# Attention followed by two gated layers on one Trainium2 core: two PSUM tiles, an earlier key preparation, and a reordered end of the attention

## The chip, the cores and the metric

The kernel runs on one core of one Trainium2 chip. Its time is device microseconds of one execution, the median of several. A profile is one execution taken by the hardware profiler; its span runs from the first instruction of the program to the last.

## What is computed

The reference chains three parts: hashed attention, a gated linear layer, and a layer of eight experts of which each token uses one.

```python
def _attn_ref(q, k, v, proj):              # 2 batches, 8 heads, 768 rows, 64 columns
    q_bits = (einsum('bhsd,dk->bhsk', q, proj) > 0)      # 6 hash bits
    k_bits = (einsum('bhsd,dk->bhsk', k, proj) > 0)
    mask = bucket(q_bits)[:, :, :, None] == bucket(k_bits)[:, :, None, :]
    scores = where(mask, scale * q @ k.T, -1e9)
    attn = softmax(scores)                                # exp(scores - max) / (sum + 1e-9)
    return attn @ v
def _moe_ref(x, w_a, w_b, w_out):           # 1536 tokens, 512 wide, 1536 hidden
    return (x @ w_a) * (x @ w_b) @ w_out
def _moe2_ref(x, expert_emb, tau, w1, w2):  # 8 experts, 512 -> 1024 -> 512
    expert_idx = argmax(normalized(x) @ normalized(expert_emb).T / tau)
    out[mask] = gate_w[mask] * (maximum(x[mask] @ w1[e], 0) @ w2[e])
```

The three `w` matrices of the gated layer come as 64-bit floats and are split in the kernel into a high and a low part; products of high and low parts are summed.

## The kernel before

**Attention** goes by 8 pairs of heads (two heads side by side on the 128 partitions) and by 48 units, six to a pair: a unit is one head's 256 query rows, taken as two score tiles t = 0 and 1 of 128 rows by 768 keys. `units` (u) numbers them; `s = u % 3` is the place within a head and `r = u % 6` within a pair. Order within each engine is the program's order, written out by hand in the loop over u of `attention`.

For each score tile `scores` multiplies q by k (fp32, L180) and adds a product of hash signs (bf16, L182) that pushes pairs of other buckets far down. `rowmax` (VectorE, L187), `expo` (ScalarE, L193, out of PSUM, so that the score buffer is free again), `normal` (GpSimd, L202 to L206) and `turn` (VectorE, a 32x32 transpose, L213) follow. There are two score buffers in PSUM (`ps_s`, four banks). The weighted sum `pv` (L222) of a head is 192 small matmuls, in two halves of 96 in the units s = 0 and s = 1; it accumulates in the other four banks, one tile `pvb`. In the unit s = 2 `epilogue` copies its two partial results (partitions 0 to 63 and 64 to 127, L240) to the SBUF tiles `xp` and `co`; `finish_add` sums them, `finish_high` and `finish_low` split the sum into `xh` and `xl`.

The same tile `pvb` serves the preparation of later pairs, in units without a weighted sum. `turned` transposes raw q and k (L107; then copies to `Q` and `K` on ScalarE, L121, and DMAs that swap the two halves of the partitions, `QS` and `KS`, L127 and L129). `signs` makes the hash products of k (L156) and q (L150) and takes their signs (`sk` L161, `qf` L151). In the unit u both parts, k then q, are issued after the scores of the next unit's first tile; their results leave PSUM in unit u + 1 behind its first exponential. `turned` of pairs 2 to 7 runs in u = 5, 11, ..., 35 and of pair 1 in u = 1, `signs` of pair 1 in u = 3 and of pairs 2 to 7 in u = 8, 14, ..., 38. In u = 41 and 44, which have no preparation, the first two of sixteen half products of the gated layer run in `pvb`'s banks (L511, via `hook`, `fill` and `gated_products`), with their results taken at once by ScalarE (L519) or VectorE (L523).

`hook(u, at)` inserts jobs of the later stages at marked places of the unit: with `plan` and `places` the loading and splitting of the first weights (`load_first`: fetch, rest, top, low, add, size, guard, parts; L409 to L442), in the tile `spare` or `late`.

**The end of the attention**: after the loop the copies of head 14 follow, then two half products, the whole weighted sum of head 15, four hooks that split weights, the last copies and ten half products. `fin == 1` and `fin == 2` in the loop put the sum of pair 6 on GpSimd and its split on ScalarE and GpSimd.

**Later stages**: the gated layer goes by chunks of 256 hidden columns (`gated_products` L511, `gated_out` L537), with routing beside the last chunk, and the experts by `hidden_rows` (L849), `hidden` (L831) and `expert_out` (L881). `begin` gives the memory of `xh` and `xl` to a pool of the experts' tiles (`xgh`, `xgl`, `hs`, `hth`, `htl`, `o`), which take their places in order of first use.

Of the kernel before, what the change touches and what calls it, by code (L numbers as in the profile page):

```python
# [25 lines left out]
class Kernel:  # L26
# [37 lines left out]
    def attention(self, xh, xl, pools, hook):  # L64
# [9 lines left out]
        for tag, shape, dt, n in (  # L74
            ("et", [128, NC * S], F32, 2), ("e", [128, S], F32, 6), ("vr", [128, NC * 256], F32, 2), ("raw", [128, 2 * S], F32, 1),
            ("q", [128, S], F32, 2), ("qs", [128, S], F32, 2), ("k", [128, S], F32, 2), ("ks", [128, H2], F32, 2),
            ("xp", [128, S], F32, 2), ("co", [128, S], F32, 2), ("qf", [128, S], BF16, 2), ("kf", [128, S], BF16, 2), ("sk", [128, H2], BF16, 1),
        ):
            sb.tile(shape, dt, tag=tag, name=tag, bufs=n)
        raw, Q, QS, K, KS, QF, KF, VR = {}, {}, {}, {}, {}, {}, {}, {}  # L80
# [18 lines left out]
        pvb = ps_pv.tile([128, 4, 512], F32, tag="pv", name="pv")  # L99

        self.banks = pvb
        self.bank = lambda: ps_s.tile([128, 2, 512], F32, tag="s", name="part")[:, 0]

        def turned(i, n):
            p = pvb[:, 2 * n:2 * n + 2]
# [12 lines left out]
            def out(eng):  # L118
# [5 lines left out]
                for a in (1, 0):  # L124
                    x, y = slice(64 * a, 64 * a + 64), slice(64 - 64 * a, 128 - 64 * a)
                    if n == 0:
                        nc.sync.dma_start(out=QS[i][x], in_=Q[i][y])  # L127
                    else:
                        nc.sync.dma_start(out=KS[i][x], in_=K[i][y, a * H2:(a + 1) * H2])  # L129
# [14 lines left out]
        def signs(i, n):  # L144
            p = pvb[:, 2 * n:2 * n + 2]
            lz = self.lz.rearrange("p a b c -> p (a b c)")
            if n == 0:
                QF[i] = sb.tile([128, S], BF16, tag="qf", name="qf", bufs=2)
# [5 lines left out]
            for x in range(2):  # L154
                r = slice(64 * x, 64 * x + 64)
# [4 lines left out]
            def out(*_):  # L160
                nc.scalar.activation(sk, p[:, 0, :H2], AF.Sign, bias=self.bias, scale=2.0 ** 100)  # L161
# [10 lines left out]
        def scores(u, t):  # L172
# [8 lines left out]
            for n, d in enumerate(rows):  # L181
                nc.tensor.matmul(st[:, n, :H2], QF[i][d, ql], KF[i][d, j], start=False, stop=True, tile_position=(64 * n, 0))  # L182
# [32 lines left out]
        def pv(h, blocks):  # L215
            et, vr = ET[h], VR[h]
            for n in blocks:
                m = 64 * (n % 2)
                v = vr[:, n % 4, n // 4 * D:n // 4 * D + D]
                for a in range(4):  # L220
                    d = slice(32 * a, 32 * a + 32)
                    nc.tensor.matmul(  # L222
                        pvb[m:m + 64, a, :NC * 32], v[d], et[d, n].rearrange("p c s -> p (c s)"),
# [3 lines left out]
        def product(n, cs):  # L227
            return pvb[64 * n:64 * n + 64, :, cs.start * 32:cs.stop * 32].rearrange("p a (c s) -> p a c s", s=32)
# [3 lines left out]
        def place(i, n, j, cs):  # L232
            if i not in XP:
                XP[i] = [sb.tile([128, S], F32, tag=t, name=t, bufs=2) for t in ("xp", "co")]
            return XP[i][n][64 * j:64 * j + 64, cs.start * 128:cs.stop * 128].rearrange("p (c a s) -> p a c s", a=4, s=32)
# [3 lines left out]
        def epilogue(h, n):  # L239
            nc.scalar.copy(place(h // 2, n, h % 2, every), product(n, every))  # L240
# [18 lines left out]
        for m in range(22):  # L259
            nc.tensor.transpose(pvb[:, m % 2, m // 2 % 4 * 128:m // 2 % 4 * 128 + 128], self.ident, self.ident)  # L260
# [4 lines left out]
        turned(0, 1)(nc.scalar)  # L265
        turned(0, 0)(nc.vector)
# [16 lines left out]
        for u in range(NU + 2):  # L283
# [4 lines left out]
            new = len(pairs)  # L288
            if act:
# [12 lines left out]
            if preps and kind is turned and held + 1 < len(pairs):  # L302
# [16 lines left out]
            if u == 1 or s == 2 and r == 5:  # L319
                new, kind = 1 if u == 1 else (u + 7) // 6, turned  # L320
            elif u == 3 or s == 2 and u > 2:
                new, kind = 1 if u == 3 else i + 1, signs
            if new < len(pairs):
                preps, held = [kind(new, x) for x in (1, 0)], new
# [20 lines left out]
        for n in range(2):  # L345
            epilogue(2 * end, n)
        hook(NU + 2, 0)
        finish_add(end, slice(0, S), slice(0, 64), nc.vector)
        pv(2 * end + 1, range(NB32))
        for at in ((NU + 2, 4), (NU + 3, 3), (NU + 3, 4), (NU + 4, 3)):  # L350
            hook(*at)
        for g in range(2):
            cs = slice(3 * g, 3 * g + 3)
            nc.scalar.copy(place(end, 1, 1, cs), product(1, cs))
            nc.vector.tensor_tensor(place(end, 0, 1, cs), product(0, cs), place(end, 1, 1, cs), ALU.add)
# [4 lines left out]
        hook(NU + 3, 0)  # L360
# [17 lines left out]
class Experts:  # L378
# [115 lines left out]
    def gated_products(self, c, t, f, which, half, psum=None):  # L494
# [22 lines left out]
        if which == 0:  # L517
            self.A = self.mid.tile([128, 384], F32, tag="a", name="a")
            nc.scalar.copy(self.A, p[:, :384])  # L519
        else:  # L520
            a = self.A
# [728 lines left out]
```

## Time and profile before

| | us |
|---|---|
| median of three runs (754.02 to 756.55) | 754.89 |
| the profiled execution | 752.32 |
| its span | 750.5 |
| busy: TensorE, VectorE, ScalarE, GpSimd | 707.7, 460.7, 351.6, 439.4 |

Attention takes up the first 245 us or so, the gated layer and the routing go to about 560, the experts to the end. The mean granted clock of TensorE is 0.993 of full speed. Matmuls are pipelined, and a matmul's recorded time reaches into the next one, so a sum of mean times is more than the time that a stream of them takes. The chain of waits follows the work that ended last back from a stretch's end; in the timeline a bracket gives the engine's idle time and what ended it.

### The profile page before, as it was taken

To read this page: it belongs to the slowest core of one execution; us is meant where nothing else is said; L and a number is where in the kernel's file an instruction comes from. 1 tells how busy PE (TensorE), PEld (TensorE's weight loads), DVE (VectorE), ACT (ScalarE), POOL (GpSimd) and SP (SyncE) were. 2 spreads that over 40 slices of the span, in tenths; PEclk is the share of its full clock that TensorE was granted. 3 is DMA by queue.
4 is the path that set the end of the run, shared out by engine and by line. 5 is a ranking of instruction groups with operands and counts; after the bars stand their busy time and mean duration, and the time that the engine had idled before them with its cause. 6 is when DMAs were issued, how large, how long until landed. Compare 5 with 4: busy or idle time off the path is not lost.

```text
span 750.5 us, 16392 instructions
## 1 busy us (share of the span) xinstructions
PE 707.7 (94%) x6793; PEld 588.6 (78%) x6793; DVE 460.7 (61%) x675; ACT 351.6 (47%) x620; POOL 439.4 (59%) x453
## 2 busy tenths in 40 slices
PE   7699898998986999999999999999999999999996
PEld 4356555555655999999999999998888999889995
DVE  3889888988785462655545646533853865565650
ACT  2667777877654344121212122224535655555551
POOL 0666888888767364462654635643612866556651
PEclk9999999999999999999999999999999999999999
DMA  6854665354215031121220211154261876666610
GB/s 145 185 118 98 135 145 124 80 118 118 72 45 179 6 114 57 56 67 48 72 97 22 91 57 57 32 207 140 72 197 38 264 235 200 242 209 232 204 67 23
DMA packets 67485, 87.62 MB, mean 117 GB/s; under 512 B 28739, under 2 KB 40003, under 8 KB 67408
## 3 DMA queue, kind: packets, MB, share of 16 engines
q1 hardware_dynamic: 63200, 78.81, 37.4%
q0 software_dynamic: 2560, 7.34, 2.6%
q8 instruction: 54, 0.88, 0.5%
q10 hardware_dynamic: 1648, 0.39, 0.3%
q14 instruction: 23, 0.19, 0.1%
HBM read 75.52 MB, written 7.34 MB: 110 GB/s over the span
## 4 chain that ended last, share of the span: by engine, by line
PE 78%; DVE 6%; ACT 5%; POOL 4%; issue 4%; DMA 2%; SPq 0%; POOLq 0%; DVEq 0%; ACTq 0%
PE ab L511 24%; PE yp L537 13%; PE op L881 10%; PE hp L831 9%; PE pv L222 6%; PE st L180 5%; DVE nm L187 2%; ACT e L193 2%; POOL e L206 2%; DVE et L213 2%; PE hr L849 2%; PE part L511 1%; PE pv L150 1%; PE st L182 1%; PE xgt L808 1%
## 5 line engine op out<-in xcount | busy, mean ns | idle before, releaser
L511 PE MATMUL ab<-xh,w 128*128 128x384 f32 x704 | 185.7, 338 | 0.0
L511 PEld LDWEIGHTS ab<-xh,w 128*128 128x128 f32 x704 | 127.7, 188 | 2.1 <-issue 1.3
L525 POOL TENSOR_TENSOR g<-a,g 128x384 fp32r<-128x384 f32 x48 | 54.7, 1140 | 109.9 <-ACT g L524 109.8
L511 PE MATMUL ab<-xl,w 128*128 128x384 f32 x352 | 118.3, 336 | 0.0
L787 POOL TENSOR_TENSOR w<-raw,w 128x1024 fp32r<-128x1024 f32 x36 | 88.0, 2448 | 36.2 <-ACT w L786 35.1
L193 ACT ACTIVATE e<-st,nm 128x768 f32<-128x768 f32 x96 | 86.5, 901 | 44.9 <-DVE nm L187 22.8
L187 DVE TENSOR_REDUCE nm<-st 128x1 f32<-128x768 f32 x96 | 90.3, 942 | 24.4 <-PE st L182 24.1
L537 PE MATMUL yp<-w,g 128*128 128x512 f32 x432 | 102.9, 390 | 0.0
L206 POOL TENSOR_SCALAR e<-e,s,mc 128x768 f32<-128x768 f32 x96 | 95.7, 1005 | 5.4 <-POOL s L204 0.2
L180 PE MATMUL st<-ks,qs 64*128 64x384 f32 x192 | 85.1, 524 | 12.0 <-ACT e L193 12.0
L213 DVE STREAM_TRANSPOSE et<-e 128x768 f32<-128x768 f32 x96 | 92.5, 964 | 4.6 <-PE pv L222 1.0
L180 PE MATMUL st<-k,q 64*128 64x384 f32 x192 | 85.3, 524 | 10.4 <-ACT e L193 10.4
L537 PEld LDWEIGHTS yp<-w,g 128*128 128x128 f32 x432 | 80.4, 188 | 14.9
L881 PE MATMUL op<-w,hth 128*128 128x512 f32 x256 | 81.7, 400 | 0.0
L831 PE MATMUL hp<-xgh,w 128*128 128x256 f32 x448 | 80.7, 281 | 0.0
L222 PE MATMUL pv<-et,vr 32*64 32x192 f32 x3072 | 72.1, 330 | 8.0 <-ACT co L240 5.3
L222 PEld LDWEIGHTS pv<-et,vr 32*64 32x64 f32 x3072 | 60.9, 133 | 23.4 <-issue 8.1
L524 ACT CAST g<-a 128x384 fp32r<-128x384 f32 x48 | 24.8, 516 | 108.3 <-DVE a L523 108.3
L787 DVE TENSOR_TENSOR w<-raw,w 128x1024 fp32r<-128x1024 f32 x28 | 64.8, 2313 | 14.6 <-ACT w L786 14.3
L831 PEld LDWEIGHTS hp<-xgh,w 128*128 128x128 f32 x448 | 69.1, 188 | 0.3
L511 PEld LDWEIGHTS ab<-xl,w 128*128 128x128 f32 x352 | 66.2, 188 | 0.8
L786 ACT CAST w<-raw 128x1024 fp32r<-128x1024 f32 x64 | 66.1, 1044 | 0.0
(197 smaller groups left out, 1162.8 us busy)
## 6 DMA issues: line engine op xcount, KB each, us to landing
raw<-in_moe_w_dram SPq DMA_DIRECT2D x32, 1024.0 KB, 5.5
vr<-in_v_dram SPq DMA_DIRECT2D x64, 192.0 KB, 4.3
raw<-in_moe_w_a_dram SPq DMA_DIRECT2D x5, 1024.0 KB, 5.2
raw<-in_moe_w_b_dram SPq DMA_DIRECT2D x5, 1024.0 KB, 5.1
raw<-in_moe_w_out_dram SPq DMA_DIRECT2D x5, 1024.0 KB, 4.9
raw<-in_k_dram SPq DMA_DIRECT2D x16, 192.0 KB, 4.7
qs<-q SPq DMA_DIRECT2D x16, 192.0 KB, 4.1
ybuf<-y SPq DMA_DIRECT2D x12, 256.0 KB, 6.3
```

The costliest lines, as they stand in the source:

```text
L180: nc.tensor.matmul(st[:, n, :H2], q[d, ql], k[d], start=True, stop=False, tile_position=(64 * n, 0))
L187: nc.vector.tensor_reduce(NM[u][:, t:t + 1], ST[u, t][:, :, :H2], axis=AX.XY, op=ALU.max, negate=True)
L193: nc.scalar.activation(e, ST.pop((u, t))[:, :, :H2], AF.Exp, bias=NM[u][:, t:t + 1], accum_out=SU[u][:, t:t + 1])
L206: nc.gpsimd.tensor_scalar(E[u, t], E[u, t], r[:, t:t + 1], c[:, t:t + 1], ALU.mult, ALU.add)
L213: nc.vector.transpose(ET[h][:, :, c], E.pop((u, t)).rearrange("p a (b s) -> p (a b) s", s=32))
L222: nc.tensor.matmul(pvb[m:m + 64, a, :NC * 32], v[d], et[d, n].rearrange("p c s -> p (c s)"), start=(n < 2), stop=(n >= NB32 - 2), tile_pos ...
L511: nc.tensor.matmul(p[:, :384], w[:, k, fs], x[:, k, cols], start=(k == 0 and n == 0), stop=(k == self.KD - 1 and n == 2),)
L537: nc.tensor.matmul(p, g[:, f, rows], w[:, f], start=(n == 0), stop=(n == 5))
L786: nc.scalar.copy(h, raw)
L787: eng.tensor_tensor(l, raw, f32(h), ALU.subtract)
L831: nc.tensor.matmul(p[:, :256], w[:, k, fs], x[:, k], start=(n == 0), stop=(n == 3 * self.KD - 1))
L881: nc.tensor.matmul(p, h[:, 2 * n + f, rows], w[:, f], start=(n == 0 and f == 0 and m == 0), stop=(n == 3 and f == 1 and m == 2),)
```

## The change

Five things, all in the order and the places of work; what is computed stays the same.

1. `pvb` becomes a list of two tiles of two banks each. K's part of a preparation uses `pvb[1]`, q's part `pvb[0]`; the weighted sum uses both. `epilogue(h, g)` copies tile g, in two pieces of 64x384, so a head has four copies, g = 1 first.
2. Where copies and a preparation meet (u = 8, 11, ..., 38), k's part (`fresh`) is issued right behind the copies of tile 1, ahead of the scores of the next unit's first tile; q's part stays where it was.
3. Apart from pair 0, the hash products of q are made like k's, in two halves of 64 columns of the array, with one sign of 128x384 to `QF` and two DMAs on SP's queue that give the other order, `QG`. Pair 0 takes four signs of 64x384 and no DMA.
4. Pair 0's transposes are both issued before their copies, and its swaps alternate between k and q. The results of the half products in u = 41 and 44 are `held` until the middle of the next unit; two further half products run in u = 48. The conversion of the output weights moves: its first half three units ahead, its second half between the steps of the end. The end puts products between the halves of the last weighted sums and takes pair 6's split behind the copies.
5. `begin` allocates the experts' tiles beforehand, with 72 floats (`edge`) between `hs` and `hth` and 56 (`room`) behind `htl`.

```diff
@@ attention: banks, swaps
-        pvb = ps_pv.tile([128, 4, 512], F32, tag="pv", name="pv")
+        pvb = [ps_pv.tile([128, 2, 512], F32, tag=f"pv{n}", name="pv") for n in range(2)]
+        def swap(i, n, a):
+            x, y = slice(64 * a, 64 * a + 64), slice(64 - 64 * a, 128 - 64 * a)
+            if n == 0:
+                nc.sync.dma_start(out=QS[i][x], in_=Q[i][y])
+            else:
+                nc.sync.dma_start(out=KS[i][x], in_=K[i][y, a * H2:(a + 1) * H2])
@@ signs
-            p = pvb[:, 2 * n:2 * n + 2]
+            p = pvb[n]
-                for x in range(2):
-                    nc.tensor.matmul(p[:, x, :H2], lz, Q[i][:, x * H2:(x + 1) * H2], start=True, stop=True)
-                return lambda *_: nc.scalar.activation(halves(QF[i]), p[:, :, :H2], AF.Sign, bias=self.bias, scale=2.0 ** 100)
+                for x, r in enumerate(half):
+                    if i == 0:
+                        nc.tensor.matmul(p[:, x, :H2], lz, Q[i][:, x * H2:(x + 1) * H2], start=True, stop=True)
+                    else:
+                        nc.tensor.matmul(
+                            p[r, 0, :H2], lz[:, r], Q[i][:, x * H2:(x + 1) * H2], start=True, stop=True, tile_position=(0, 64 * x)
+                        )
+                def out(*_):
+                    if i == 0:
+                        for x in range(2):
+                            sign(QF[i][half[x]], p[half[x], x, :H2])
+                            sign(QG[i][half[1 - x]], p[half[1 - x], x, :H2])
+                        return
+                    sign(QF[i], p[:, 0, :H2])
+                    for x in range(2):
+                        nc.sync.dma_start(out=QG[i][half[1 - x]], in_=QF[i][half[x]])
@@ scores
+                qf = (QF if n == c // (NC // 2) else QG)[i][d, c % (NC // 2) * 128:c % (NC // 2) * 128 + 128]
@@ copies
-        def epilogue(h, n):
-            nc.scalar.copy(place(h // 2, n, h % 2, every), product(n, every))
+        def epilogue(h, g):
+            for n in range(2):
+                nc.scalar.copy(place(h // 2, n, h % 2, g, every), product(n, g, every))
@@ start
-        turned(0, 1)(nc.scalar)
-        turned(0, 0)(nc.vector)
+        turns = turned(0, 1), turned(0, 0)
+        turns[0](nc.scalar, False)
+        turns[1](nc.vector, False)
+        for a in (1, 0):
+            for n in (1, 0):
+                swap(0, n, a)
@@ loop over the units
-            moves = [((u - 8) // 3, n) for n in range(2)] if s == 2 and u >= 8 else []
+            moves = [((u - 8) // 3, g) for g in (1, 0)] if s == 2 and u >= 8 else []
             for m in moves[:2 if u == NU - 1 else 1]:
                 epilogue(*m)
+            if moves and new < len(pairs):
+                fresh.append(kind(new, 1))
...
-                preps, held = [kind(new, x) for x in (1, 0)], new
+                preps, held, held_kind = fresh + [kind(new, x) for x in (1, 0)[len(fresh):]], new, kind
...
-                    if fin == 1:
+                    if fin == 2:
                         finish_add(done, cols[g])
-                    if fin == 2:
-                        finish_high(done, cols[g])
-                        finish_low(done, cols[g])
@@ end
-        for n in range(2):
-            epilogue(2 * end, n)
+        for g in (1, 0):
+            epilogue(2 * end, g)
         hook(NU + 2, 0)
+        hook(NU + 2, 3)
+        pv(2 * end + 1, range(12))
         finish_add(end, slice(0, S), slice(0, 64), nc.vector)
-        pv(2 * end + 1, range(NB32))
-        for at in ((NU + 2, 4), (NU + 3, 3), (NU + 3, 4), (NU + 4, 3)):
-            hook(*at)
+        finish_high(end - 1, slice(0, S))
+        hook(NU + 2, 4)
+        hook(NU + 3, 0)
+        pv(2 * end + 1, range(12, NB32))
+        for g in range(3):
+            finish_low(end - 1, cols[g])
+        hook(NU + 3, 3)
...
-        hook(NU + 3, 0)
+        hook(NU + 4, 0)
@@ tile_kernel: hooks and pool
-            fill = {41: 2, 44: 2, NU + 2: 2, NU + 3: 10}
+            fill = {41: 2, 44: 2, NU: 2, NU + 2: 2, NU + 3: 2, NU + 4: 6}
             def hook(u, at):
+                if at == 3:
+                    while held:
+                        held.pop(0)()
...
+            for tag, n in (("xgh", 1024), ("xgl", 1024), ("hs", 1024), ("edge", 72), ("hth", 2048), ("htl", 2048), ("room", 56)):
+                X.ex.tile([128, n], F32, tag=tag, name=tag, bufs=1)
```

## Rows read from the trace of the kernel before

**Rows 1.** Busy time by stretch: stretch, us, busy us (instructions) of each engine, clock, DMA.

```profile
140.00:180.00 40.00, 36.17 (x727) 22.57 (x733) 34.33 (x48) 29.79 (x55) 34.22 (x58) 1.00 0.49 110
...
400.00:500.00 100.00, 100.00 (x533) 94.28 (x532) 52.06 (x69) 22.00 (x39) 54.04 (x29) 1.00 0.25 85
```

**Rows 2.** Unit 35: one line of the timeline, then the chain of waits (start, us, what).

```profile
169.28 0.79 ACT L240 COPY xp<-pv 64x768 f32<-64x768 f32 x1 [0.96 <-PE pv L222]
...
172.33 0.96 DVE nm L187
...
175.07 0.71 ACT q L121
...
175.82 2.21 PE pv L222 x96
```

**Rows 3.** The chain of waits through unit 38.

```profile
182.09 0.79 ACT xp L240
...
184.91 0.80 PE pv L156 x4
...
185.70 1.49 PE pv L150 x4
...
187.19 0.84 PE st L180 x4
...
188.20 0.64 PE st L180 x4
...
189.01 1.00 PE pv L222 x40
```

**Rows 4.** Groups by shape, attention: busy us, mean ns of one, idle before.

```profile
L354 ACT COPY co<-pv 64x384 f32<-64x384 f32 x2 | 1.0, 476 | 1.3 <-PE pv L222 0.7 <-DVE xp L355 0.6
```

**Rows 5.** Timeline of unit 39: an exponential and what it waited for.

```profile
186.00 0.90 ACT L193 ACTIVATE e<-st,nm 128x768 f32<-128x768 f32 x1 [0.38 <-DVE r L197]
```

**Rows 6.** Timeline of the start: start, us, engine, line, operation, [idle before, releaser].

```profile
8.66 0.88 PE L107 MATMUL pv<-ident,raw 128*128 128x128 f32 x6 [0.90 <-ACT k L121]
...
13.14 0.58 ACT L161 ACTIVATE sk<-pv,bias 128x384 bf16<-128x384 f32 x1 [4.53 <-PE pv L150]
...
14.95 1.82 DVE L187 TENSOR_REDUCE nm<-st 128x1 f32<-128x768 f32 x2 [0.64 <-PE st L182]
```

**Rows 7.** DMA issues: tile, queue, count, KB each, median us to landing.

```profile
ks<-k SPq DMA_DIRECT2D x16, 96.0 KB, 2.2
```

**Rows 8.** Units 41 to 46: the chain's product, then the timeline.

```profile
198.39 2.30 PE pv L511 x12
...
200.71 0.48 ACT L519 COPY a<-pv 128x384 f32<-128x384 f32 x1 [1.68 <-PE pv L511]
...
214.61 0.56 DVE L523 TENSOR_TENSOR a<-pv,a 128x384 f32<-128x384 f32 x1 [2.42 <-PE pv L511]
...
217.20 0.59 PE L180 MATMUL st<-ks,qs 64*128 64x384 f32 x1 [1.68 <-ACT e L193]
```

**Rows 9.** Timeline of attention's end.

```profile
226.13 4.12 PE L222 MATMUL pv<-et,vr 32*64 32x192 f32 x181 [0.76 <-ACT co L240]
...
230.67 3.79 DVE L213 STREAM_TRANSPOSE et<-e 128x768 f32<-128x768 f32 x4
...
231.29 0.57 PE L222 MATMUL pv<-et,vr 32*64 32x192 f32 x11 [1.04 <-issue]
...
235.40 0.41 ACT L248 CAST xh<-xp 128x256 fp32r<-128x256 f32 x1 [4.07 <-POOL xp L244]
...
238.74 5.65 PE L222 MATMUL pv<-et,vr 32*64 32x192 f32 x192 [4.58 <-ACT co L240]
```

**Rows 10.** Busy time in the last weighted sum, with the granted clock.

```profile
238.50:241.50 3.00, 2.76 (x72) 2.38 (x80) 2.32 (x4) 1.01 (x3) 0.63 (x2) 0.50 0.88 309
```

**Rows 11.** The page's groups of the later stages: busy us, mean ns.

```profile
L537 PE MATMUL yp<-w,g 128*128 128x512 f32 x432 | 102.9, 390 | 0.0
...
L881 PE MATMUL op<-w,hth 128*128 128x512 f32 x256 | 81.7, 400 | 0.0
```

More of the change, by code (lines that the diff above doesn't have):

```diff
@@ L116, in turned, with out @@
             dst = halves((Q, K)[n][i])
-            def out(eng):
+            def out(eng, swaps=True):
                 scale = float(D) ** -0.5 if n == 0 else 1.0
@@ L123, in out @@
                     eng.tensor_scalar(dst, p[:, :, :H2], scale, None, ALU.mult)
[L124 to L129, printed above, removed]
+                if swaps:
+                    for a in (1, 0):
+                        swap(i, n, a)
             return out
@@ L181, in scores @@
             for n, d in enumerate(rows):
[L182 removed]
+                qf = (QF if n == c // (NC // 2) else QG)[i][d, c % (NC // 2) * 128:c % (NC // 2) * 128 + 128]
+                nc.tensor.matmul(st[:, n, :H2], qf, KF[i][d, j], start=False, stop=True, tile_position=(64 * n, 0))
         def rowmax(u, t):
@@ L288, in attention @@
             new = len(pairs)
+            if u == 1 or s == 2 and r == 5:
+                new, kind = 1 if u == 1 else (u + 7) // 6, turned
+            elif u == 3 or s == 2 and u > 2:
+                new, kind = 1 if u == 3 else i + 1, signs
+            fresh = []
             if act:
@@ L301, in attention @@
                 prep(nc.scalar)
-            if preps and kind is turned and held + 1 < len(pairs):
+            if preps and held_kind is turned and held + 1 < len(pairs):
                 load(held + 1)
@@ L491, in load_first, with gated_products @@
         return self.split64(src, shape, dest, scratch)
-    def gated_products(self, c, t, f, which, half, psum=None):
+    def gated_products(self, c, t, f, which, half, psum=None, held=None):
         nc = self.nc
@@ L516, in gated_products, with out @@
             return
-        if which == 0:
-            self.A = self.mid.tile([128, 384], F32, tag="a", name="a")
-            nc.scalar.copy(self.A, p[:, :384])
-        else:
-            a = self.A
-            gh, gl = self.G[c, t]
-            nc.vector.tensor_tensor(a, p[:, :384], a, ALU.mult)
-            nc.scalar.copy(gh[:, f], a)
-            nc.gpsimd.tensor_tensor(gl[:, f], a, f32(gh[:, f]), ALU.subtract)
+        def out():
+            if which == 0:
+                self.A = self.mid.tile([128, 384], F32, tag="a", name="a")
+                nc.scalar.copy(self.A, p[:, :384])
+            else:
+                a = self.A
+                gh, gl = self.G[c, t]
+                nc.vector.tensor_tensor(a, p[:, :384], a, ALU.mult)
+                nc.scalar.copy(gh[:, f], a)
+                nc.gpsimd.tensor_tensor(gl[:, f], a, f32(gh[:, f]), ALU.subtract)
+        if held is None:
+            out()
+        else:
+            held.append(out)
     def gated_out(self, c, t, m):
@@ L1057, in hook @@
                         if half == 0:
-                            X.part = K.banks[:, (2 if u == 44 else 0) + n // 2] if u < NU else K.bank()
-                        X.gated_products(0, t, f, w, half, X.part)
+                            X.part = K.banks[(2, 0)[n // 2]] if u < NU else K.bank()
+                        X.gated_products(0, t, f, w, half, X.part, held if u < NU else None)
             K.attention(X.xh, X.xl, (sb, ps_s, ps_pv), hook)
```

51 lines of the change are left out of this document (28 added, 23 removed).

## The prediction

> **What bounds the kernel now.** I read the busy times by stretch first. From about 260 us on TensorE never rests [rows 1]: that part shifts as a whole, and a microsecond saved before it is a microsecond saved at the end, unless the change alters a matmul there. In the attention TensorE is busy 36.2 of 40 us, VectorE 34.3 and GpSimd 34.2 (140 to 180 us in [rows 1]), so three engines stand close together and only the waits that end last can be won. Next I read the chain of waits through the two kinds of unit in which a preparation follows the copies of the weighted sums.
>
> In a unit with transposes (pair 7's, u = 35) the chain runs over ScalarE and VectorE, not over TensorE: first copy at 169.28, row maximum of the next unit at 172.33, its exponential, the copy of k, the copy of q to 175.78, and only then the next weighted sum at 175.82 [rows 2]: 6.54 us. In a unit with hash products (u = 38) the first copy starts at 182.09, the exponential follows, then scores, K hash 0.80, Q hash 1.49, scores, and the weighted sum follows TensorE's own work without a wait at 189.01 [rows 3]: 6.92 us.
>
> **The change part by part.** The sum is made against the profiled execution: span 750.5 us, time 752.32, which is 2.57 below the median of the three runs (754.89). I subtract the gains from the median.
>
> *Hash and transposes in the copy units.* The two copies of 64x768 become four of 64x384: one took 0.476 us [rows 4] against 0.79 [rows 2, 3], so two take 0.95 where one took 0.79, 0.16 more ahead of the exponential. Step by step for hash units (u = 8, 14, 20, 26, 32, 38), counted from the first copy: bank pair 1 is free at 0.95; K hash runs 0.95 to 1.80; the exponential (0.90 [rows 5] and a release) ends at 1.89; the scores end at 2.98, 0.16 later than now, where the K hash stands behind them at 2.82 [rows 3]; Q hash, now two products side by side like K's, 0.80 instead of 1.49 [rows 3], to 3.8; the second exponential ends near 3.8 too, so the next scores start there, 1.2 earlier than now. But the exponential after it starts now at 186.00, held by its row maximum [rows 5], 3.91 after the first copy; it can only move to 4.07, as its scores moved by 0.16. It ends at 5.07; then the two signs, now 0.58 each, as the sign of K in [rows 6], about 0.48 apart, to 6.15. The weighted sum starts at 6.2 instead of 6.9: 0.7 each, at most. In some of these units VectorE also splits weights and its maximum comes later still, which leaves nothing; no gain in two of the six is my allowance, and I take 0.5 x 6 = 3.0 us (ends: 6 x 0.16 lost, 6 x 1.2 gained if the scores' lead lasted to the weighted sum).
>
> In transpose units (u = 11, 17, 23, 29, 35) the same steps end at the copy of q, which is last on ScalarE as before; TensorE's earlier scores buy nothing, because the chain of [rows 2] goes over the exponential. They lose the 0.16, or nothing if the copies overlap a little; taken 0.1 x 5 = 0.5 lost (ends: 0.8 lost, 5 x 0.4 gained). The Trainium skill (ScalarE: Activation LUTs, What ACT_TABLE_LOAD costs) says that activations back to back overlap by about 93 ns. In [rows 2] the copies of k and q do stand closer (0.71) than one of them lasts; by that rule two short copies would take 0.86, and the eleven units together would be 1.0 us better than summed here.
>
> *Q hash of pair 1* (u = 3, no copies there): the pipeline is filling and the scores behind it are awaited, so 0.69 comes off (L150 less L156 in [rows 3]): 0.7, at worst 0.
>
> *The swap of the query signs.* The second half order of the signs is now made by two DMAs on SP's queue, 48 KB each. The nearest row, K's swap with 96 KB, lands in 2.2 us [rows 7]; pair 7's signs are made ahead of the weighted sum at 189.01 [rows 3], and its first scores stand just ahead of the product at 198.39 [rows 8]: some 8 us of lead. Queued behind the DMAs on SP are only the next loads of v, a unit later. Cost 0, with that lead as cover. Pair 1 has the shortest lead, a unit and a half, behind loads of q and k: 0 to 0.5.
>
> *The start.* Today the query transposes wait 0.90 for the copy of k, although they write other banks, and the sign of K waits 4.53 for the query hash [rows 6]: one tile, one dependency. With two tiles the query's copy ends 0.9 earlier, the K hash runs beside it instead of behind it (0.8), so the Q hash ends about 1.8 earlier. Now two signs stand between it and the first scores, 13.14 to about 14.5; then there are four of 64x384, of which the first scores need two (about 1.0) if halves are tracked apart, all (2.0) if not. K's and Q's swaps alternate, so that the halves read first are issued first. The first row maximum (14.95 in [rows 6]) comes 1.3 to 2.1 earlier: 1.6.
>
> *Two gated products held back* (u = 41, 44). ScalarE waits 1.68 in order for the first, VectorE 2.42 for the second, and the exponential held up behind it costs TensorE 1.68 [rows 8]. Moved past the next row maximum, both waits have cover. The first shows no such wait of TensorE behind it; I give it a quarter of its 1.68: 0.4 + 1.5 = 1.9 (ends 0.5 and 3.4). The first half of the output weights is converted three units earlier: a 512 KB load on SP, four VectorE, two ScalarE and two GpSimd steps that now lie in u = 42 to 45. I take 0 for it, up to 1.0 if GpSimd, which has only some 14% idle, falls behind.
>
> *The end.* Between 226.13 and the end of the last weighted sum, 238.74 + 5.65 = 244.39, TensorE has 18.26 us [rows 9]. ScalarE waits there 4.07 for GpSimd's sum before it can cast, and the copies behind this cast release the last weighted sum, 4.58 late; after that the granted clock is 0.50, which is 1.2 GHz [rows 10]: 192 matmuls take 5.65, though half as many take 2.21 [rows 2]. The change takes the cast out of the way and puts products between the halves. The work in that stretch is 4 x 2.21 + 2.30 (twelve products [rows 8]) = 11.14; the others only change places. The copies cost 0.2 once more: 18.26 - 11.14 - 0.2 = 6.9, taken 6.8. Both covers hold: four copies (1.9) lie under the products (2.3), and the last weighted sum would start near 235.3 on today's clock while the last transpose ends at 234.5 [rows 9]. What is late next is TensorE itself. The unexplained pause of 1.04 [rows 9] may come again, as may the low clock (1.2) and a late transpose (1.5): lower end 3.0.
>
> *Room in the experts' pool.* 72 floats ahead of hth move it and htl by 288 bytes. `yp` and `op` have one shape, yet last 390 and 400 ns [rows 11], so where operands lie may matter. 384 such matmuls by 10 ns are 3.8 us either way; nothing says which. I take 1.0 gained, nearer to no change.
>
> Sum: 1.6 + 0.7 + 3.0 - 0.5 + 1.9 + 6.8 + 1.0 = 14.5 off: 754.9 - 14.5 = 740.4 us (737.8 for an execution like the profiled one).
>
> **The rivals.** *ScalarE and VectorE keep the copy units* (chance 0.16): rows 2 and 5 speak for it, the hash units' last wait on TensorE against. All eleven lose 0.16: the 2.5 gained turn into 1.8 lost, a time of 744.7.
>
> *The end does not close* (0.12): GpSimd's backlog, which the moved conversions only shift, holds the last normalization, so that the end gives 2 instead of 6.8: 745.2. For it: GpSimd is 4.07 late there already [rows 9]. Against: its conversions then lie earlier.
>
> *Changing the array's tiling* (0.06): scores that follow other scores take 0.64, after a hash 0.84 [rows 3], so a change costs 0.20. The change splits each preparation in two: two more such changes in eleven units. I count none, since a wait stands at each; if not, 22 x 0.20 = 4.4 us: 744.8. The Trainium skill (TensorEngine Tiling, Key Properties) says that switching the tiling mode, not merely the tile, drains TensorE; the difference in [rows 3] agrees in direction, and by this rule the price is paid wherever TensorE has no wait to hide it.
>
> *Slower: the two tiles are still waited for as one* (0.04). The K part then waits for all four copies, the last of them behind the exponential, and it stands ahead of the scores on TensorE: it would start 2.8 after the first copy instead of 0.95, and the scores behind it, and with them the chain, 1.9 later. Eleven units lose 20.9, against 12.0 gained elsewhere: 763.8. It decides once the K part waits over 1.3 us longer than computed. Against it: [rows 6] show waits within one tile, and these are two.
>
> **How the numbers follow.** Forecast 0.60, around 740.4 (own range 735 to 746 from the ends above); ScalarE and VectorE 0.16; the end 0.12; tiling 0.06; slower 0.04; the remaining 0.02 are several losses together, near no change. Every case but the last two is faster by more than 0.3% (2.3 us, about what a measurement of this kernel can tell from no change): faster 0.94, same 0.02, slower 0.04. The range 734 to 748 takes in the rivals near 745 and leaves the combinations out.
>
> **What would show it.** Right: query transposes at about 7.8; first row maximum at 12.9 to 13.6; hash units 6.2 us from first copy to weighted sum, transpose units still 6.6; no wait of ScalarE or VectorE for a product at u = 41 and 44; no idle TensorE and no low clock between 226 and 250. Wrong: a K part that starts after all four copies, scores that wait for the swapped signs, or `op` matmuls that last other than 400 ns by more than the 2.6 ns I took.

## The result

The kernel after takes 738.61 us (median, 737.05 to 739.98), the kernel before 755.12 in the same call: ratio 0.9782, 95% interval 0.9766 to 0.9799, 16.5 us less. The forecast of 740.4 and its range held. The profiled executions have spans of 735.3 and 750.5 us, 15.2 apart; all terms below are differences between these two traces unless another is named, and "head" is the time from the first matmul of one head's weighted sum to that of the next. One run below, `one_tile`, was traced in an execution of 795.15 us whose mean granted clock was 0.85; neither this time nor this trace is used, and the same kernel was run once more.

Where the 15.2 us are:

| stretch | before | after | gain | predicted |
|---|---|---|---|---|
| to the first row maximum | 14.95 | 13.02 | 1.93 | 1.6 |
| from there to the first weighted sum | 27.41 | 25.86 | 1.55 | 0.7 |
| six heads with a hash unit (8, 14, ... 38) | 79.02 | 75.69 | 3.33 | 3.0 |
| five heads with a transpose unit (11, ... 35) | 67.56 | 66.34 | 1.22 | -0.5 |
| heads with units 41, 44 and 47 | 37.19 | 37.01 | 0.18 | 1.9 |
| last but one weighted sum to the first yp matmul | 28.70 | 23.08 | 5.62 | 6.8 |
| first yp matmul to the end | 495.7 | 494.3 | 1.4 | 1.0 |

The other 1.3 of the 16.5 us lie in executions of which there is no trace: the traced execution of the kernel before was 2.8 us below its median, that of the kernel after 1.6.

The start, in the timeline of the kernel after (start, us, engine, line, operation, idle before it and its releaser), to be held against [rows 6]:

```profile
6.57 1.50 PE L114 MATMUL pv<-ident,raw 128*128 128x128 f32 x12 [1.11 <-DMA raw<-in_k_dram]
7.45 0.81 ACT L128 ACTIVATE k<-pv 128x768 f32<-128x768 f32 x1 [3.38 <-PE pv L114]
8.36 0.87 PE L181 MATMUL pv<-k,lz 128*64 128x384 f32 x4 [0.29 <-issue]
9.27 0.58 ACT L154 ACTIVATE sk<-pv,bias 128x384 bf16<-128x384 f32 x1 [1.01 <-PE pv L181]
11.94 0.56 PE L205 MATMUL st<-ks,qs 64*128 64x384 f32 x1 [0.38 <-DMA qs<-q]
13.02 1.82 DVE L213 TENSOR_REDUCE nm<-st 128x1 f32<-128x768 f32 x2 [2.58 <-PE st L208]
```

All twelve transposes run in one piece, and the sign of K starts as K's hash ends. Of the 1.93 us, 0.34 are not the change's: the rows of k landed earlier in this execution (first transpose at 6.57 against 6.91). From the first transpose to the first row maximum it is 8.04 before and 6.45 after (6.44 to 6.55 in the nine other traces with two tiles and this start), 1.59 less. Unit 38, a hash unit, in the same timeline, against [rows 3]:

```profile
174.66 0.47 ACT L268 COPY xp<-pv 64x384 f32<-64x384 f32 x1 [0.46 <-PE pv L248]
175.15 0.48 ACT L268 COPY co<-pv 64x384 f32<-64x384 f32 x1
175.67 0.87 PE L181 MATMUL pv<-k,lz 128*64 128x384 f32 x4
...
177.70 0.87 PE L163 MATMUL pv<-q,lz 128*64 128x384 f32 x4
...
180.22 0.58 ACT L154 ACTIVATE qf<-pv,bias 128x384 bf16<-128x384 f32 x1
...
180.91 0.90 PE L248 MATMUL pv<-et,vr 32*64 32x192 f32 x31
```

From the first copy to the weighted sum 6.25 us (6.2 were computed), ended by the sign of the query hash. In the same timeline of the kernel before it is 6.85, since the weighted sum starts here:

```profile
188.94 1.38 PE L222 MATMUL pv<-et,vr 32*64 32x192 f32 x54
```

The 6.92 of the prediction is from the chain of waits, which puts this start at 189.01. The two copies stand 0.49 apart and last 0.47 and 0.48. The Trainium skill (ScalarE: Activation LUTs, What ACT_TABLE_LOAD costs) has ACTIVATE instructions back to back overlap by about 93 ns; these COPY instructions don't, and the 1.0 us that this rule would have given is not there.

The end, against [rows 9] and [rows 10]; TensorE's weighted sums alone:

```profile
217.92 2.21 PE L248 MATMUL pv<-et,vr 32*64 32x192 f32 x96 [1.09 <-ACT co L268]
...
222.35 1.85 PE L248 MATMUL pv<-et,vr 32*64 32x192 f32 x73
225.01 0.88 PE L248 MATMUL pv<-et,vr 32*64 32x192 f32 x23 [0.80 <-issue]
...
228.10 2.21 PE L248 MATMUL pv<-et,vr 32*64 32x192 f32 x96
```

The last weighted sum starts at 228.10 and 232.52 in two halves, at full clock (2.21 for 96 matmuls). What is left idle is the wait for the copies and a pause of 0.80 within a weighted sum.

### The profile page after: what moved, and what is told of

It is laid out like the page before. It is cut to its first block, busy times and chain, and to the rows that moved or that the text cites. A ratio compares the mean times of both kernels' runs of the same rounds, so it can differ in the third digit from the quotient of the medians.

```text
span 735.3 us, 16440 instructions
## 1 busy us (share of the span) xinstructions
PE 702.2 (96%) x6793; PEld 582.2 (79%) x6793; DVE 463.3 (63%) x675; ACT 353.4 (48%) x651; POOL 440.6 (60%) x453
## 4 chain that ended last, share of the span: by engine, by line
PE 78%; DVE 7%; ACT 4%; issue 4%; DMA 4%; POOL 2%; SPq 1%; POOLq 0%; DVEq 0%; ACTq 0%
PE ab L548 24%; PE yp L580 13%; PE op L924 10%; PE hp L874 10%; PE pv L248 8%; PE st L205 5%; DVE nm L213 3%; ACT e L219 2%; DVE et L239 2%; PE part L548 2%; PE hr L892 2%; DMA vr<-in_v_dram 1%; PE xgt L851 1%; PE st L208 1%; DMA raw<-in_k_dram 1%
## 5 line engine op out<-in xcount | busy, mean ns | idle before, releaser
L557 ACT COPY a<-ab 128x384 f32<-128x384 f32 x44 | 21.0, 478 | 94.6 <-PE ab L548 93.2
```

## The experiments

Each was timed in five rounds beside the kernel before on the same chip. The kernel before had medians of 753.9 to 754.2 us in these calls, so times are compared by their ratio to it; 0.3% is what they can tell apart, and the stretches of the traces tell more.

### The start: one tile

```diff
-        pvb = [ps_pv.tile([128, 2, 512], F32, tag=f"pv{n}", name="pv") for n in range(2)]
+        whole = ps_pv.tile([128, 4, 512], F32, tag="pv", name="pv")
+        pvb = [whole[:, 2 * n:2 * n + 2] for n in range(2)]
```

> The kernel after with one PSUM tile of four banks in place of two of two banks; the program is the same otherwise, so that only what is waited for differs. Theory: two tiles are worth something at the start alone, where the query transposes then wait for the copy of k and the signs for both hashes: 1.3 to 1.9 us lost, about 740.2 us. Rival: K's part in the eleven copy units waits for all four copies too, about 1.2 us or more in each: 752 us or more.

Measured 741.65 us, ratio 0.9825 (0.9794 to 0.9856).

> The same kernel as one_tile, for its trace and a second set of times. Theory: in the trace the query transposes wait about 0.9 us for the copy of k and the signs for the hash products of the other part, so the first row maximum comes at 14.6 to 15.2 us instead of 13.0 to 13.4; from the first weighted sum on, the eleven copy units take what they take in the kernel after (142 us from the first weighted sum of head 0 to that of head 11), since K's part is issued ahead of the other two copies. Time about 1.7 above the kernel after. Rival: in the units too the K part waits for all copies: 150 us or more for that stretch.

Measured 741.32 us, 0.9836 (0.9815 to 0.9856). The start of its timeline:

```profile
8.21 0.81 ACT L129 ACTIVATE k<-pv 128x768 f32<-128x768 f32 x1 [4.13 <-PE pv L115]
9.05 0.96 DVE L131 TENSOR_SCALAR q<-pv 128x768 f32<-128x768 f32 x1 [1.56 <-ACT k L129]
10.15 0.87 PE L182 MATMUL pv<-k,lz 128*64 128x384 f32 x4 [1.98 <-DVE q L131]
10.95 2.58 PE L162 MATMUL pv<-q,lz 128*128 128x384 f32 x4
13.57 0.58 ACT L155 ACTIVATE sk<-pv,bias 128x384 bf16<-128x384 f32 x1 [4.55 <-PE pv L162]
...
15.64 0.96 DVE L214 TENSOR_REDUCE nm<-st 128x1 f32<-128x768 f32 x1 [0.91 <-PE st L209]
```

The copies wait for each other's transposes, K's hash for the copy of q, the sign of K for Q's hash. First row maximum at 15.64: 2.6 later than after, of which 0.1 is a later landing of k and 1.0 is Q's hash, 2.58 instead of 1.56, at a low granted clock (mean 0.58 from 10.9 to 13.5 us). So two tiles are worth 1.5 to 2.5 there. From the first weighted sum to that of the twelfth head it takes 141.9 us, after 142.0: in the eleven copy units one tile costs nothing, as K's part is issued ahead of the copies that it doesn't need. The slower rival (763.8) falls.

### The copy units: which part earns

The halves of the query hash alone, on the kernel before (the swaps and four signs for pair 0 as in the change):

```diff
-                    nc.tensor.matmul(p[:, x, :H2], lz, Q[i][:, x * H2:(x + 1) * H2], ...)
+                    nc.tensor.matmul(p[r, 0, :H2], lz[:, r], Q[i][:, x * H2:(x + 1) * H2], ..., tile_position=(0, 64 * x))
```

> The kernel before with one part of the change alone: the query hash products in column halves, one sign of 128x384 and two swaps by DMA (one tile, old order, old end). Theory: the hash units end on TensorE, so 0.69 us comes off in each of six, and 0.7 in pair 1's, 4.8 us together: 750.3 us against 755.1. Rival (the chain over ScalarE and VectorE holds the units): only pair 1's 0.7, 754.4 us.

Measured 749.13 us, 0.9925 (0.9898 to 0.9952). Its start is longer than before, first row maximum at 16.64 instead of 14.95, with the hash products at a low clock (mean 0.59 from 10.7 to 14.5 us), so the whole time says less than the stretches.

K's part behind the scores, on the kernel after:

```diff
-            if moves and new < len(pairs):
-                fresh.append(kind(new, 1))
```

> The kernel after with K's part of each preparation put back behind the next scores (K and Q parts together, as before); two tiles, halves and everything else stay. Theory: in the copy units TensorE waits for the exponential, and K's part fills that wait; put back, about 0.4 us is lost in each of six hash units and 0.5 in each of five transpose units: 4.9 us, 743.5 us. Rival (ScalarE and VectorE keep these units): nothing is lost, 738.6 to 739.1 us.

Measured 741.58 us, 0.9825 (0.9797 to 0.9853). The heads say it (us):

| | six hash heads | five transpose heads |
|---|---|---|
| before | 79.02 | 67.56 |
| halves alone | 74.85 | 67.93 |
| after, K's part behind the scores | 76.00 | 68.19 |
| after (two traces) | 75.69, 75.86 | 66.34, 66.20 |

The halves give the hash heads 4.2. From the second line to the third the hash heads lose 1.15: 0.29 to 0.31 in four of them, nothing in two. Two copies become four there (0.16 a unit were computed), but the second tile comes in as well, so that the copies are the cause is argued, not shown. K's part ahead gives the hash heads 0.1 to 0.3 and the transpose heads 1.85 to 2.0. Neither theory had it: 2 us lie between the rival's 0 to 0.5 and the 4.9. Where they lie shows in the weighted sum after unit 14, with K's part behind the scores:

```profile
79.07 2.21 PE L248 MATMUL pv<-et,vr 32*64 32x192 f32 x96
...
80.13 0.82 DVE L449 TENSOR_SCALAR spare<-spare 128x512 int32<-128x512 int32 x1
...
80.86 0.94 DVE L213 TENSOR_REDUCE nm<-st 128x1 f32<-128x768 f32 x1
...
82.94 0.59 PE L205 MATMUL st<-ks,qs 64*128 64x384 f32 x1 [0.66 <-ACT e L219]
```

and in the kernel after:

```profile
77.19 2.21 PE L248 MATMUL pv<-et,vr 32*64 32x192 f32 x96
...
77.77 0.39 DVE L451 TENSOR_SCALAR spare<-spare 128x512 int32<-128x512 int32 x1
...
78.07 0.95 DVE L213 TENSOR_REDUCE nm<-st 128x1 f32<-128x768 f32 x1
...
80.24 0.51 PE L205 MATMUL st<-ks,qs 64*128 64x384 f32 x1
```

Both units take 6.3 us from the first copy to the weighted sum. But with K's part ahead the scores of the unit come sooner, VectorE gets ahead, and its next row maximum starts 0.88 us after the weighted sum instead of 1.79. The scores behind the sum then wait for no exponential. The lead is paid out one unit later, in the head that I counted as a transpose head. It is not the same in every head: 1.46 of the 1.85 are in two of the five (0.55 in the second head, 0.91 in the fourth, which is shown here), the other three gain 0.06 to 0.17. And of the 0.91 us by which this row maximum starts sooner only half is the lead itself; the rest is the step of the weight conversion ahead of it, which lasts 0.39 here and 0.82 there. What lengthens that step is not shown.

### The experts' pool

```diff
-        for tag, n in (("xgh", 1024), ("xgl", 1024), ("hs", 1024), ("edge", 72), ("hth", 2048), ("htl", 2048), ("room", 56)):
+        for tag, n in (("xgh", 1024), ("xgl", 1024), ("hs", 1024), ("hth", 2048), ("htl", 2048)):
```

> The kernel after without the two blocks of room (72 and 56 floats) in the experts' pool; nothing else differs. Theory: where hth lies sets the pace of the op matmuls, so they go back from 227 to about 234 ns from start to start and from 396 to 400 ns each, and the time from 738.6 to about 740.1 us, all of the 1.4 behind the first yp matmul. Rival: the room does nothing and the 1.4 there is something else: 738.6, op as in the kernel after.

Measured 740.11 us, 0.982 (0.9794 to 0.9846), which alone tells little. The page's group of the op matmuls does, for the kernel after:

```profile
L924 PE MATMUL op<-w,hth 128*128 128x512 f32 x256 | 80.8, 396 | 0.0
```

and without the room:

```profile
L924 PE MATMUL op<-w,hth 128*128 128x512 f32 x256 | 81.7, 400 | 0.0
```

From the first op matmul to the end of the last it is 184.20 us after, 185.38 without the room, 185.64 before. 1.2 of the 1.4 us are the place of two tiles.

### Held products and the moved conversion

```diff
-                        X.gated_products(0, t, f, w, half, X.part, held if u < NU else None)
+                        X.gated_products(0, t, f, w, half, X.part, None)
```

> The kernel after with the results of the two gated products of units 41 and 44 taken at once instead of behind the next row maximum. Theory of the prediction: 1.9 us are lost, 740.5 us. Rival, from the trace of after: the conversion of the output weights that was moved beside unit 44 holds the row maximum there anyway, so only the 0.7 of unit 41 is lost: 739.3 us.

Measured 741.51 us, 0.9828 (0.9802 to 0.9854). The heads of units 41 and 44 take 14.20 and 16.69, after 13.47 and 15.26: 2.2 us, so the theory's 1.9 and not the rival's 0.7. VectorE waits for the product again, and TensorE behind it:

```profile
208.54 0.56 DVE L561 TENSOR_TENSOR a<-pv,a 128x384 f32<-128x384 f32 x1 [2.23 <-PE pv L548]
...
211.73 0.82 PE L205 MATMUL st<-ks,qs 64*128 64x384 f32 x1 [2.28 <-ACT e L219]
```

After that gap the clock is 0.50 (columns: stretch, us, busy us of PE, PEld, DVE, ACT, POOL, clock, DMA share, GB/s), and the next head takes 0.87 more:

```profile
212.00:215.20 3.20, 3.20 (x54) 1.72 (x60) 2.87 (x5) 2.05 (x5) 3.01 (x5) 0.50 0.03 5
```

So holding the products is worth what was predicted, but in the kernel after unit 44 is no shorter than before. The timeline of after shows why:

```profile
205.40 1.22 DVE L473 SCALAR_TENSOR_TENSOR late<-late 128x512 f32<-128x512 f32 x1 [1.09 <-POOL late L462]
...
206.54 0.94 DVE L213 TENSOR_REDUCE nm<-st 128x1 f32<-128x768 f32 x1
...
208.63 0.59 PE L205 MATMUL st<-ks,qs 64*128 64x384 f32 x1 [1.05 <-ACT e L219]
```

The guard of the moved conversion stands ahead of the row maximum. One unit later:

```diff
-                (42, 43, 43, 44, 44, 44, 45),
+                (42, 43, 43, 44, 44, 45, 46),
```

> The kernel after with the last two steps of the moved conversion (VectorE's guard and the split into parts) one unit later, guard in unit 45 and parts in 46. Theory: the guard, which waits 1.09 us for GpSimd at 205.40 and stands ahead of unit 45's row maximum, costs TensorE the gap of 1.05 there; one unit later GpSimd's sum is long ready, and about 0.9 us comes off: 737.7 us. Rival: VectorE has no room in unit 45 either, the wait only moves: 738.6 us.

Measured 738.57 us, 0.9804 (0.9775 to 0.9834); the heads tell the two apart, and it is the rival.

```profile
210.26 1.17 DVE L473 SCALAR_TENSOR_TENSOR late<-late 128x512 f32<-128x512 f32 x1
211.35 0.94 DVE L213 TENSOR_REDUCE nm<-st 128x1 f32<-128x768 f32 x1
...
213.43 0.59 PE L205 MATMUL st<-ks,qs 64*128 64x384 f32 x1 [1.03 <-ACT e L219]
```

The guard now waits for nothing and costs the same: unit 44's head falls to 13.91, the next rises from 8.28 to 9.55. Its price is its own length on VectorE, not GpSimd's lateness. But that length is not fixed. With GpSimd at work beside it the guard takes 1.17 to 1.22 in units 44 and 45 of these traces; in `products_at_once`, where GpSimd was idle meanwhile, it took 0.68:

```profile
209.02 0.68 DVE L473 SCALAR_TENSOR_TENSOR late<-late 128x512 f32<-128x512 f32 x1
```

No run tests what lengthens it.

The copies, at units 41 and 44:

```diff
+            lead = 2 if u == NU - 1 else 0 if moves and new == len(pairs) else 1
-            for m in moves[:2 if u == NU - 1 else 1]:
+            for m in moves[:lead]:
...
-            for m in moves[2 if u == NU - 1 else 1:]:
+            for m in moves[lead:]:
```

> The kernel after with all four copies of the weighted sums behind the first exponential in units 41 and 44, where no preparation waits for them. Theory: the two copies ahead of the exponential (0.96 us) are the whole of TensorE's gaps of 1.13 there, since the row maximum was ready before the copies began; both gaps close, 1.9 us less: 736.7 us. Rival: the second exponential, now behind four copies, is late instead and the gain is lost: 738.6 us.

Measured 738.38 us, 0.9793 (0.9764 to 0.9822). The head of unit 41 takes 12.25 instead of 13.47, that of 44 15.85 instead of 15.26; TensorE's waits move to the next exponential. The rival, but for 0.6. The theory's premise held in unit 41 alone: there the row maximum ended at 186.85, ahead of the copies at 187.18; in unit 44 it ended at 201.63, after the copies had begun at 201.16.

### The end

```diff
+                    if fin == 1:
+                        finish_add(done, cols[g])
                     if fin == 2:
-                        finish_add(done, cols[g])
+                        finish_high(done, cols[g])
+                        finish_low(done, cols[g])
...
-        hook(NU + 2, 3)
-        pv(2 * end + 1, range(12))
         finish_add(end, slice(0, S), slice(0, 64), nc.vector)
-        finish_high(end - 1, slice(0, S))
...
-        pv(2 * end + 1, range(12, NB32))
...
+        pv(2 * end + 1, range(NB32))
+        for at in ((NU + 2, 3), (NU + 2, 4), (NU + 3, 3)):
+            hook(*at)
...
-            fill = {41: 2, 44: 2, NU: 2, NU + 2: 2, NU + 3: 2, NU + 4: 6}
+            fill = {41: 2, 44: 2, NU + 2: 2, NU + 3: 10}
```

> The kernel after with the order of attention's end as before (the last but one pair's sum, cast and remainder early in ScalarE's and GpSimd's order, the last weighted sum in one piece, the products behind it); the conversions of the output weights stay early. Theory: the stretch from the last but one weighted sum to the first yp grows back by 5.6 us to 28.7, with the wait of ScalarE for GpSimd's sum and the half clock in the last weighted sum: 744.2 us. Rival: what held the end was GpSimd's backlog of conversions, which stays moved: about 2 us lost, 740.6 us.

Measured 741.42 us, 0.9841 (0.981 to 0.9873). The stretch takes 26.90 us, 3.8 more than after and 1.8 less than before: both theories hold a part. With the conversions early the wait of 4.58 ahead of the last weighted sum is gone, though ScalarE still waits 3.40 for GpSimd's sum. What remains is TensorE's pause and the clock behind it (timeline, then two stretches):

```profile
218.66 4.12 PE L248 MATMUL pv<-et,vr 32*64 32x192 f32 x181 [1.09 <-ACT co L268]
225.39 0.93 PE L248 MATMUL pv<-et,vr 32*64 32x192 f32 x11 [2.61 <-issue]
```

```profile
219.00:224.70 5.70, 3.78 (x181) 3.44 (x166) 4.12 (x6) 2.02 (x6) 5.34 (x10) 1.00 1.05 299
224.70:231.60 6.90, 6.21 (x55) 5.09 (x62) 2.32 (x4) 3.66 (x8) 3.40 (x5) 0.51 0.58 194
```

The pause comes after the 181st matmul of the weighted sum, as before [rows 9], and after has it within the same sum. I had called it unexplained. In the DMA view of after from 222 to 225 us there is one packet on the queue that loads instructions, among two weight loads that fill the engines:

```profile
DMA  6979999999999997999999999999999798653222
...
q1 hardware_dynamic: 518, 1.02, 89.8%
q8 instruction: 1, 0.02, 2.2%
```

That gave a test, with a cure for the guard in it:

```diff
-            plan = {..., (37, 1): [outs[0][0]], (47, 1): [outs[1][0]]}
+            plan = {..., (37, 1): [outs[0][0]], (49, 1): [outs[1][0]]}
-                (42, 43, 43, 44, 44, 44, 45),
+                (42, 43, 43, 44, 44, 48, 49),
```

> The kernel after, unchanged, on the chip of the next two: 738.6 us; the pause of TensorE inside the second half of the last but one weighted sum (after its 73rd matmul) 0.8 to 1.4 us, as in the kernels that share this order.

Measured 739.57 us, 0.9799 (0.9774 to 0.9825); pause 1.21.

> The kernel after with guard and parts of the moved conversion taken out of units 44 and 45 into 48 and 49, where no row maximum follows, and the 512 KB load of the second half of the output weights, which needs the same buffer, put behind them into unit 49; SP issues the 1024 KB load of the next weights behind it. Theory 1: the guard's own 1.2 us on VectorE is what TensorE's gap of 1.05 in units 44 and 45 consists of, and it goes. Theory 2: TensorE's pause after the 73rd matmul is the fetch of its next block of instructions, which in the trace shares the DMA engines at 97 to 101% with these two loads; with both loads later it shrinks below 0.3 us. Together 1.6 us less than the kernel after in the same call, 737.0. Rivals: the gap moves to the last transposes again (no gain), the pause is TensorE's own and stays 0.8 or more (1.0 less, 737.6); the first yp matmul waits for the late weights (up to 2 us more).

Measured 736.32 us, 0.9763 (0.9739 to 0.9787). The second half of the same weighted sum, and the DMA view from 220 to 222 us:

```profile
222.67 2.21 PE L248 MATMUL pv<-et,vr 32*64 32x192 f32 x96
```

```profile
DMA  9599993758635329000000000000000000000000
...
q1 hardware_dynamic: 86, 0.11, 28.9%
q8 instruction: 1, 0.02, 4.0%
```

The block of instructions comes as soon as the loads of v are done, and the weighted sum has no pause. The packets' own times in the traces say the same (us; "after its end" is from the end of the packet to the next matmul):

| kernel | packet of instructions | TensorE goes on | after its end |
|---|---|---|---|
| before | 228.91 to 229.93 | 231.29 | 1.36 |
| after | 222.61 to 223.66 | 225.01 | 1.35 |
| after_again | 225.45 to 226.53 | 227.90 | 1.37 |
| end_as_before | 222.90 to 223.99 | 225.39 | 1.40 |
| copies_behind | 223.63 to 224.69 | 226.16 | 1.47 |
| late_load | 220.75 to 222.02 | no pause | |

In the six other traces used here that have a pause (1.11 to 1.47 us long) it ends 1.23 to 1.46 us after the packet, so over all eleven it is 1.23 to 1.47. In `late_load` TensorE passes the same matmul 2.17 us after its packet, and doesn't stop; in `late_load_copies` it comes there 1.25 after the packet (222.07 to 223.25) and goes on at 1.45, a stop of 0.2.

But the weight loads are not the only thing that makes the packet late. In the kernel before they are issued at 234.72, behind the pause. There the packet comes at 228.91, as the loads of v end (DMA share 0.82 to 1.05 from 226 to 228.9 us, 0.12 in the next 1.1), and TensorE, which has no products to do in this stretch, is at the point of the pause by 230.25, 0.3 us after the packet. So what counts is how long before that point the packet lands.

Against `after_again`, unit 44's head falls from 15.23 to 13.91 and the end from 23.48 to 22.33. Both theories hold; the first yp matmul waits for no late weights (ahead of it TensorE idles 0.29 once). The Trainium skill (Runtime: NRT & Kernel Launch, Instruction fetch mechanics) says that an engine fetches its instructions by DMA in blocks of 16 KiB and that this is mostly hidden. The packet of 0.02 MB agrees; that it is hidden holds at this place in `late_load` alone, where the packet landed 2.17 us before it was needed.

The last run adds this to `late_load`:

```diff
-            for m in moves[:2 if u == NU - 1 else 1]:
+            lead = 0 if moves and new == len(pairs) else 1
+            for m in moves[:lead]:
...
+            hook(u, 5)
...
-                if at == 0:
+                if at == (5 if u == NU else 0):
```

> As late_load, and besides all copies of the weighted sums behind the first exponential in units 41, 44 and 47, and the two products that followed the first half of the last but one weighted sum put ahead of it, into TensorE's wait of 1.09 us for the copies. Theory: 0.6 us comes off in unit 41 and 0.6 in 44, whose gap behind the copies has no guard on top any more, 0.95 at the end: some 2.2 us less than late_load, 734.8. Rival: the second exponential of each unit is late instead, which leaves 0.5: 736.5.

Measured 735.99 us, 0.9755 (0.9732 to 0.9777), not told apart from `late_load`; from the twelfth head's weighted sum to yp 57.66 us against 58.16. The rival. Both versions beat the kernel after (739.57 in their call) by 0.4%.

## Why the prediction was right, and where not

The total is closer than its terms: 14.5 forecast against 15.2 in the traces, with the transpose heads 1.7 and pair 1 0.85 above their terms and the heads of units 41 to 47 1.7 and the end 1.2 below. That these cancel is luck. The part behind 260 us is also not quite without rest, as I read from [rows 1]: TensorE is busy there 482.34 of 485 us before.

*The start* (1.6, measured 1.93): right in mechanism and size, 1.59 without the earlier landing of k; at 11.94 the scores now wait 0.38 for the swapped query rows.

*Pair 1* (0.7): the halves alone shortened this stretch from 27.41 to 26.60, both with a low clock for a time. The other half of the 1.55 is luck: the profiled execution before has the clock at 0.50 for a time here, after at 1.00. `after_again`, the same program as after, needs 28.09 us for it, with two such times (same columns as above), and the other traces with this part of the change 26.49 to 28.19; so what the change is worth here is not told apart from the clock. The two times in `after_again`:

```profile
25.90:29.00 3.10, 3.10 (x10) 1.19 (x12) 2.93 (x6) 1.02 (x3) 2.08 (x4) 0.50 1.08 227
36.00:39.20 3.20, 3.20 (x17) 2.26 (x13) 3.07 (x6) 2.24 (x6) 2.25 (x5) 0.50 0.00 0
```

*The swap of the query signs* (0, for pair 1 up to 0.5): too low. SP issues pair 1's swap behind four loads of q and k, at 30.59 in after, where it costs nothing, and at 32.96 in `late_load`, with the same start of the program:

```profile
32.96 1.64 SPq L175 DMA_DIRECT2D qg<-qf  x2
...
36.66 0.33 PE L208 MATMUL st<-kf,qg 64*128 64x384 bf16 x1 [1.76 <-DMA qg<-qf]
```

In `guard_later` it is 0.97, in `products_at_once` 0.25. Scores that wait for the swapped signs were named as a sign of being wrong; it came, in these three runs. The row I priced it by, K's swap [rows 7], was a median of all pairs, not of the one behind those loads.

*Hash units* (3.0, measured 3.33): right in size, and in unit 38 by its own steps: the weighted sum ends up behind ScalarE's signs. Two allowances cancel: no unit gained nothing, as I had allowed for two, but none gained the 0.7 either. From first copy to weighted sum five of the six units gained 0.53 to 0.59, u = 26 0.25. And the gain is the halves' (4.2 in heads) less what the rest of the change took, which the prediction did not part.

*Transpose units* (-0.5, measured +1.22): the unit was right, the account was not. From first copy to weighted sum the five units grew from 34.10 to 34.29 us. But I let the lead of the scores end with the unit, "TensorE's earlier scores buy nothing", while `k_behind_scores` shows that a lead won in the hash unit comes out behind it, 1.9 us over five heads, most of it in two.

*Held products* (1.9): 2.2 by `products_at_once`, right. *The moved conversion* (0, up to 1.0) was the mis-sized term: 1.3 in unit 44 by `late_load`. I looked at GpSimd's room; VectorE had none, and the guard counted with its own length in both places ahead of a row maximum. In unit 47, 0.35 went as well: four copies of 0.48 stand there where two of 0.79 stood. These three make about 0.5, where the heads gained 0.18; the rest is open.

*The end* (6.8, measured 5.6): mechanism right, 1.2 too large: the pause was listed as a lower end, and came at 0.80; the wait for the copies is 1.09 instead of 0.76. The reorder gave 3.4 to 3.8 of it, 1.4 to 1.8 of that by a shorter pause (0.80 and 1.21 against 2.61). The other 1.8 came with the rest of the change; that it is the moved conversions was not tested, and the prediction did not part the two.

*The pool* (1.0, measured 1.2 by `no_room`): luck. The sign was a guess, and no run gives a reason for it. The 4 ns by which the op matmuls are shorter are more than the 2.6 that the prediction set as its limit.

The rivals: the chain over ScalarE did keep the transpose units, but not what lay behind them; the end closed; changes of tiling cost nothing that shows, since the heads with copy units gained 4.5 us where that rival had them lose 1.9, though no run tests them alone.

## What to carry to other kernels

Count a moved step from one start of the repeating work to the next, not within the unit in which it moved: a lead that another engine seems to eat can come out a unit later. On an engine without spare time, a step ahead of a reduction that others wait for cost its own length in both places of the loop where it was tried, so place it where no such reduction follows. Look where a burst of loads meets a long run of short matmuls: the engine's own instructions come through the same DMA engines.

## What was not expected of the hardware

A pause inside a run of independent matmuls, called "issue", was the load of the next instructions: 0.80, 1.21 and 2.61 us with loads of v and of weights on the DMA engines, 1.04 before with loads of v alone, none in `late_load`, with products between the halves and the weights behind. TensorE's waits of 2.28 and 2.61 us were each followed by a granted clock of 0.50, which is 1.2 GHz. 288 bytes of shift of hth changed an fp32 matmul of unchanged shape from 400 to 396 ns; why is open, and so is what sets the 390 of `yp`, whose operands did not move. Why one execution has the low clock early in attention and another of the same program hasn't is open too; with it the stretch from the first row maximum to the first weighted sum took 28.09 us in `after_again`, without it 25.86 in after.
